# Sliding-window attention into a SwiGLU block: masks by a scan, loads further ahead and tied to the score matmuls, an order of the opening written anew

## The chip, the core and the metric

The kernel runs on one core of a Trainium2 chip. The metric is the time of one execution on the device in microseconds (us), here the median of 16 runs. The core has engines that run side by side, each with its own queue of instructions: TensorE (PE; its weight loads are shown as PEld), VectorE (DVE), ScalarE (ACT), GpSimd (POOL) and SyncE (SP). POOL, SP and ACT also issue DMAs. Engines wait for each other through semaphores, and each works its queue off in order: an instruction that waits holds up all that stand behind it.

## The reference

q, k and v have 8 batches, 8 heads, 576 positions and head size 64. Attention is causal with a window of 64:

```
scores = q @ k^T / 8        kept where 0 <= i - j < 64, else -1e9
attn   = exp(scores - max) / sum;   x = attn @ v     -> as 4608 tokens x 512
out    = (silu(x @ w_gate) * (x @ w_val)) @ w_out    w_gate, w_val: 512 x 1536, w_out: 1536 x 512
```

Inputs and output are float32; the kernel works in bf16 with float32 sums, and may do so.

## The kernel before

The 4608 tokens are cut into 36 attention chunks n of 128 tokens and 9 chunks c of 512 tokens for the SwiGLU block. A chunk n passes through these steps, each a method of the class:

- `load(n)` (line 271): POOL issues three DMAs (six where a chunk crosses a batch) that fetch k, q and v from memory and cast them to bf16: `kn`, `qn` (rings of `NQ` = 6) and `va` (a ring of `NV` = 10). The weights come the same way (`load_w`, `load_wo`).
- the transposes of k and q, which need the head dimension on the partitions. For chunks 0 to 7 PE does them (`first_T`, `Tpe`) and DVE and ACT copy the results out of PSUM; from chunk 8 on `T(n, "k")` and `T(n, "q")` (line 323) are DMA transposes that SP issues. k ends in `kT`, which holds all tokens; q in `qT`, a ring of `NZ` = 8.
- `shift_v(n)`: two DMAs on SP (or DVE copies at the start) that place v shifted by 64 rows, `vb`.
- `S(n)` (line 339): 16 small matmuls for the scores into two PSUM banks, then exp on ACT and, if no bias is used, a multiplication with `mask` on DVE. For chunks 0 to 3 (`bias=True`) two matmuls with `nmask` (0 or -30000) put the mask into PSUM instead.
- `AV(n)`: attention times v, into two banks; DVE divides (`rc`, `xb`).
- `X(n)` (line 402): x is transposed into `xT`, by a DMA transpose on SP, or, with `eng` "act" or "dve", by PE into a bank that this engine copies out.

`F(c, f, lo, hi)` is one of 12 steps of the SwiGLU block: four matmuls of x with a block of w_gate, tanh on ACT, four with a block of w_val, and two DVE operations that write `hT` (silu is made from tanh; the factor is 0.5). At the opening F works on halves of 256 tokens (lo to hi), as soon as two chunks of x are there. `O(c, u)` is 12 matmuls of `hT` with w_out, a copy on ACT and a store. PSUM has eight banks: F rotates over 0 to 3, O uses 4, and all of attention and of PE's transposes ("a") rotates over 5 to 7; `banks()` changes a rotation.

The order of work is written out by hand. `opening()` and `build()` call these methods one after the other; that order is the order on every engine's queue. `_Graph` adds a semaphore wait wherever an operation needs data of, or overwrites data that is still read by, an earlier one. From `for c in range(2, NFC)` on (line 708) the order is a loop of 28 steps u: three F, an AV, a T, an X, an S, an O and a load six chunks ahead. Each group of 12 F closes with four chunks of x, and F(c, 0) needs all four.

The masks are built in `init()` and `init_mask` (line 261): DVE fills `nmask` and `mask` with a constant, and POOL cuts the window with two affine selects and a memset each, in its queue between the DMA issues.

Of the kernel before, what the change touches and what calls it, by code (L numbers as in the profile page):

```python
# [149 lines left out]
class _Kernel:  # L150
    NQ = 6
# [14 lines left out]
    def alloc(self):  # L166
# [21 lines left out]
        self.wz = sb("wz", 512)  # L188
        self.pt = [t[:, :].rearrange("p (h x) -> p h x", h=H) for t in ring("pt", self.NP, H * 192)]
# [47 lines left out]
    def init(self):  # L237
        g = self.g
        self.zero(self.wup[:, :], ["wup"])
        g.op("act", lambda e: e.activation(self.wup[:, :], self.wup[:, :], ACTF.Exp), writes=["wup"])  # L240
        self.zero(self.ident[:, :], ["ident"])
        self.zero(self.wz[:, :], ["wz"])
        self.zero(self.nmask[:, :], ["nmask"])
        self.init_va(0, 4)
        self.zero(self.kT[:, :, 0:64], [("kT", -1, 0), ("kT", -1, 1)])
        self.zero(self.vb[0][0:64, :, 0:66], [("vb", 0, 0)])
        for i in range(self.NP):
            self.zero(self.pt[i][:, :, 64:128], [("pt", i, 0), ("pt", i, 1)])
        self.zero(self.mask[:, :], ["mask"], 1.0)
        self.init_va(4, self.NV)  # L250

# [9 lines left out]
    def init_mask(self, m, key, fill):  # L261
        mm = m[:, :].rearrange("p (a q) -> p a q", a=4)
        self.g.op("pool", lambda e: e.affine_select(
            out=mm, in_=mm, compare_op=ALU.is_gt, fill=fill, base=0,
            pattern=[[0, 4], [-1, 64]], channel_multiplier=1), writes=[key])
        self.g.op("pool", lambda e: e.affine_select(
            out=mm, in_=mm, compare_op=ALU.is_ge, fill=fill, base=64,
            pattern=[[0, 4], [1, 64]], channel_multiplier=-1), writes=[key])
        self.g.op("pool", lambda e: e.memset(m[0:64, 128:192], fill), writes=[key])

    def load(self, n, what="kqv"):
        if n >= NCH:
            return
        parts = list(self.segs(128 * n, 128))
        for x in what:
# [7 lines left out]
            for j, (r, b, s, L) in enumerate(parts):  # L283
                d = dst[r:r + L, :, 0:64]
                a = src[b, :, s:s + L, :].rearrange("h p d -> p h d")
                ks = [(nm, i, j)] if len(parts) > 1 else [(nm, i, 0), (nm, i, 1)]
                self.g.op("pool", lambda e, d=d, a=a: e.dma_start(d, a), writes=ks, dma=True)  # L287
# [51 lines left out]
    def S(self, n, bias=False):  # L339
# [26 lines left out]
        g.op("pe", pe, reads=rd, writes=[b[1] for b in bx])  # L366
# [210 lines left out]
    def opening(self):  # L577
        W = lambda a, b: (self.load_w("g", a, b), self.load_w("v", a, b))
        g = self.g
        self.first_loads()  # L580
        self.init()
        self.init_ident(self.ident, "ident")
# [3 lines left out]
        self.init_mask(self.nmask, "nmask", -30000.0)  # L586
# [4 lines left out]
        W(2, 3)  # L591
        W(3, 4)
        self.init_mask(self.mask, "mask", 0.0)
# [7 lines left out]
        self.load(6)  # L601
        self.load(7)
        self.load_wo(0, 6)
        self.load_wo(6, 12)
        for n in range(4, 8):
            self.shift_v(n)
# [15 lines left out]
        self.AV(1)  # L622
        self.banks("a", [5, 6, 7, 4])
        self.X(0, "act")
        self.S(2, True)
        self.X(1, "dve")
        self.shift_v(2, "dve")
        self.F(0, 0, 0, 256)
        self.AV(2)
        self.Tpe(3, ("dve", "act"))  # L630
        self.F(0, 1, 0, 256)
        self.X(2, "act")
        self.S(3, True)
        self.shift_v(3, "dve")
        self.F(0, 2, 0, 256)
        self.F(0, 3, 0, 256)
        self.AV(3)
        self.F(0, 4, 0, 256)
        self.X(3, "act")
        self.F(0, 5, 0, 256)  # L640
        for f in range(6):
            self.F(0, f, 256, 512)

    def build(self):
        self.opening()
        self.banks("a", [5, 6, 7])
# [16 lines left out]
        for n in (8, 9, 10):  # L663
            self.load(n)
        for n in (8, 9, 10):
            self.T(n, "k")
            self.T(n, "q")
            self.shift_v(n)
        for f in range(0, 8):
            self.F(1, f, 0, 256)  # L670
            if f == 0:
                self.S(6)
            if f == 2:
                self.AV(6)
                self.S(7)
            if f == 4:
                self.X(6, "act")
                self.AV(7)
            if f == 6:
                self.X(7, "act")  # L680
        for f in range(0, 8):
            self.F(1, f, 256, 512)
            if f == 1:
                self.load(11)
            if f == 4:
                self.O(0, 0)
                self.S(8)
            if f == 5:
                self.O(0, 1)
                self.load(12)  # L690
            if f == 6:
                self.AV(8)
                self.X(8)
        self.S(9)
        self.load(13)
        for u in range(4):
            self.F(1, 8 + u)
            self.T(11 + u, "k")
            if u < 2:
                self.O(0, 2 + u)  # L700
            if u < 3:
                self.AV(9 + u)
                self.X(9 + u)
                self.S(10 + u)
            self.T(11 + u, "q")
            self.shift_v(11 + u)
            self.load(14 + u)
        for c in range(2, NFC):
            for u in range(4):
# [7 lines left out]
                self.load(n + 6)  # L717
                self.F(c, 3 * u + 1)
                self.S(n + 1)
                late = c == NFC - 1 and u == 3  # L720
# [52 lines left out]
```

## Time and profile before

| | |
|---|---|
| median of 16 runs | 358.28 us (355.09 to 360.06) |
| profiled execution, its own time | 357.74 us |
| span, from first to last instruction of it | 356.0 us |
| PE busy | 330.4 us, 93% of the span |
| DVE busy | 222.7 us, 63% |
| ACT busy | 136.7 us, 38% |
| POOL busy | 115.0 us, 32% (issuing DMAs of this queue counts as busy) |
| mean granted TensorE clock | 0.981 |

The profile gives for each engine the busy time, and for groups of instructions the mean duration of one, the idle time of the engine before them and what ended it. The timeline lists instructions in order of time, and writes [idle before <-releaser] behind those that the engine stood still for. "Issue to landing" of a DMA is the time from its issue until its data are there. Times inside the profile are counted from the start of the span.

### The profile page before, as it was taken

The numbers are of one execution on the slowest core, as the hardware profiler recorded it, in microseconds if no ns is written. First come the engines' busy times: TensorE is split into PE (matmuls) and PEld (weight loads), VectorE is DVE, ScalarE is ACT, GpSimd is POOL, SyncE is SP. The second block draws the span as 40 slices with busy tenths as digits, with TensorE's granted clock in tenths as the row PEclk, the third lists the DMA queues.
The fourth block names the chain that finished last, engine by engine and source line by source line (L and its number), as shares of the span: only waits on it lengthen the run. The fifth ranks groups of instructions, "written<-read, shape, count | busy, mean of one in ns | idle before, by whom it ended". The sixth has DMA issues, their size and how long they took to land.

```text
span 356.0 us, 6815 instructions
## 1 busy us (share of the span) xinstructions
PE 330.4 (93%) x2648; PEld 174.2 (49%) x2689; DVE 222.7 (63%) x493; ACT 136.7 (38%) x248; POOL 115.0 (32%) x147
## 2 busy tenths in 40 slices
PE   7899879985769999999999999999999999999996
PEld 2677458652334444444444444444444444444443
DVE  8778878463536666666666666666666666555520
ACT  3555445332314444433333333333444334332321
POOL 8999976521453433232323422210000000000000
PEclk9899999998789999999999999999999999999999
DMA  9999999999999999999999999894433321110012
GB/s 175 150 157 181 182 210 157 157 195 167 181 165 168 143 147 138 123 143 135 149 145 139 153 139 154 126 142 99 96 93 92 94 55 44 64 41 29 31 57 92
DMA packets 177600, 45.47 MB, mean 128 GB/s; under 512 B 162144, under 2 KB 173088, under 8 KB 177568
## 3 DMA queue, kind: packets, MB, share of 16 engines
q0 software_dynamic: 119424, 18.36, 77.9%
q1 hardware_dynamic: 51920, 16.84, 28.1%
q10 hardware_dynamic: 6224, 9.83, 8.1%
q8 instruction: 21, 0.34, 0.4%
q14 instruction: 11, 0.09, 0.1%
HBM read 37.75 MB, written 9.44 MB: 133 GB/s over the span
## 4 chain that ended last, share of the span: by engine, by line
PE 83%; DVE 7%; ACT 4%; DMA 3%; issue 3%; ACTq 0%; DVEq 0%
PE ps L496 48%; PE ps L542 26%; PE ps L359 3%; DVE uu L515 2%; DVE xb L399 2%; ACT sig L507 2%; DMA xT<-xb 2%; PE ps L390 2%; PE ps L389 2%; DMA hT<-in_k_dram 1%; DVE hT L518 1%; ACT pt L372 1%; PE ps L564 1%; PE ps L418 1%; PE ps L353 1%
## 5 line engine op out<-in xcount | busy, mean ns | idle before, releaser
L515 DVE SCALAR_TENSOR_TENSOR uu<-sig,ps 128x512 bf16<-128x512 bf16 (+1 forms) x122 | 76.0, 623 | 93.9 <-ACT sig L507 93.5
L496 PE MATMUL ps<-xT,Wg 128*128 128x512 bf16 (+1 forms) x474 | 112.3, 358 | 6.0 <-DMA xT<-xb 3.7
L496 PE MATMUL ps<-xT,Wv 128*128 128x512 bf16 (+1 forms) x476 | 114.8, 359 | 1.4 <-DMA Wv<-in_moe_w_val_dram 0.8
L507 ACT ACTIVATE sig<-ps 128x512 bf16<-128x512 f32 (+1 forms) x122 | 66.9, 549 | 101.2 <-PE ps L496 101.1
L542 PE MATMUL ps<-Wo,hT 128*128 128x512 bf16 x405 | 94.1, 379 | 1.4 <-issue 1.0
L518 DVE SCALAR_TENSOR_TENSOR hT<-uu,ps 128x512 bf16<-128x512 bf16 (+1 forms) x122 | 76.3, 626 | 5.0 <-PE ps L496 0.8
L496 PEld LDWEIGHTS ps<-xT,Wv 128*128 128x128 bf16 x488 | 48.2, 99 | 48.2 <-issue 2.2
L496 PEld LDWEIGHTS ps<-xT,Wg 128*128 128x128 bf16 x488 | 44.8, 99 | 44.4 <-DMA xT<-xb 4.2
L287 POOL DMA_DIRECT2D qn<-in_q_dram x38 | 33.9, 897 | 88.3 <-DMA qT<-qn 88.3
L542 PEld LDWEIGHTS ps<-Wo,hT 128*128 128x128 bf16 x420 | 39.2, 98 | 44.9
L372 ACT ACTIVATE pt<-ps 128x512 bf16<-128x512 f32 x72 | 39.0, 595 | 30.0 <-PE ps L359 29.6
L547 ACT ACTIVATE ost<-ps 128x512 f32<-128x512 f32 x35 | 20.9, 597 | 67.1 <-PE ps L542 67.1
L287 POOL DMA_DIRECT2D kn<-in_k_dram x38 | 34.2, 903 | 27.5 <-DMA kT<-kn 26.1
L287 POOL DMA_DIRECT2D va<-in_v_dram x40 | 35.9, 902 | 3.4 <-DMA Wo<-in_moe_w_out_dram 2.6
L399 DVE TENSOR_TENSOR xb<-ps,rc 128x256 bf16<-128x256 f32 x72 | 30.6, 424 | 2.5
L374 DVE TENSOR_TENSOR pt<-pt,mask 128x512 bf16<-128x512 bf16 x64 | 24.9, 420 | 10.6 <-ACT pt L372 10.1
L390 PE MATMUL ps<-va,pt 128*128 128x65 bf16 x288 | 23.4, 196 | 0.0
L389 PE MATMUL ps<-vb,pt 128*128 128x65 bf16 x288 | 23.3, 196 | 0.0
L389 PEld LDWEIGHTS ps<-vb,pt 128*128 128x128 bf16 x288 | 21.0, 100 | 4.0 <-issue 0.6
L359 PE MATMUL ps<-qT,kT 64*128 64x64 bf16 x576 | 14.9, 192 | 7.6 <-issue 4.0
L390 PEld LDWEIGHTS ps<-va,pt 128*128 128x128 bf16 x288 | 19.7, 100 | 3.7 <-issue 0.5
L359 PEld LDWEIGHTS ps<-qT,kT 64*128 64x128 bf16 x576 | 10.6, 95 | 21.0 <-DVE rc L396 10.4
(51 smaller groups left out, 88.0 us busy)
## 6 DMA issues: line engine op xcount, KB each, us to landing
out_dram<-ost ACTq DMA_DIRECT2D x35, 256.0 KB, 3.1
vb<-va SPq DMA_DIRECT2D x63, 80.0 KB, 4.6
va<-in_v_dram POOLq DMA_DIRECT2D x32, 128.0 KB, 6.2
kn<-in_k_dram POOLq DMA_DIRECT2D x30, 128.0 KB, 6.4
qn<-in_q_dram POOLq DMA_DIRECT2D x30, 128.0 KB, 5.4
Wo<-in_moe_w_out_dram POOLq DMA_DIRECT2D x2, 768.0 KB, 13.9
Wg<-in_moe_w_gate_dram POOLq DMA_DIRECT2D x6, 128.0 KB, 4.6
Wv<-in_moe_w_val_dram POOLq DMA_DIRECT2D x6, 128.0 KB, 4.6
```

The costliest lines, as they stand in the source:

```text
L287: self.g.op("pool", lambda e, d=d, a=a: e.dma_start(d, a), writes=ks, dma=True)
L359: r = e.matmul(sv[p][:, w, c], self.kT[ps, c, k0:k0 + 128], self.qT[ps, c, self.qs(n, 64 * w, 64 * w + 64)], start=not bias, stop=not bias ...
L372: g.op("act", lambda e, po=po, p=p: e.activation(po, sv[p], ACTF.Exp, scale=SCALE), reads=[bx[p][1]], writes=[pk])
L374: g.op("dve", lambda e, po=po: e.tensor_tensor(po, po, m, ALU.mult), reads=[pk, "mask"], writes=[pk])
L389: e.matmul(av[:, j, :], pt[:, h, 0:128], vb[:, h, 0:65], start=True, stop=False)
L390: r = e.matmul(av[:, j, :], pt[:, h, 64:192], va[:, h, 0:65], start=False, stop=True)
L399: g.op("dve", lambda e, xo=xo, av=av, rb=rb: e.tensor_tensor(xo, av[:, :, 0:64], rb, ALU.mult), reads=[bk, ("rc", ir)], writes=[("xb", ix, ...
L496: r = e.matmul(bank[:, lo:hi], W[:, kk, f * 128:f * 128 + 128], xT[:, kk, lo:hi], start=(kk == 0), stop=(kk == NK - 1))
L507: self.g.op("act", lambda e: e.activation(sig[:, lo:hi], G[:, lo:hi], ACTF.Tanh, scale=0.5), reads=[gk], writes=[("sig", i)])
L515: g.op("dve", lambda e: e.scalar_tensor_tensor(uu[:, lo:hi], sig[:, lo:hi], 1.0, G[:, lo:hi], ALU.add, ALU.mult), reads=[("sig", i), gk], ...
L518: g.op("dve", lambda e: e.scalar_tensor_tensor(hT[:, f, lo:hi], uu[:, lo:hi], 0.5, V[:, lo:hi], ALU.mult, ALU.mult), reads=[("uu", i), vk] ...
L542: r = e.matmul(OB[:, :], hT[:, f, 128 * u:128 * u + 128], self.Wo[:, f, :], start=(f == 0), stop=(f == NF - 1))
```

## The change

- **Masks.** `nmask` and `mask` are no longer made on POOL. DVE makes a running sum along each row of the identity (a scan), takes the difference of two halves of it, clears one corner, and makes `nmask` from `mask` by one more operation. Two memsets on DVE go.
- **Weights.** Blocks 2 and 3 of each gate matrix come with one DMA instead of two.
- **Opening.** The order of X, F, S and Tpe in the first 512 tokens is another; X(0), X(1) and F(0,0) come ahead of S(2), X(3) stands behind F(0,5). The loads 6 and 7, w_out and the shifts of v 4 to 7 stand later in the text, but in the same order on POOL and SP.
- **Banks.** The attention rotation keeps four banks (5, 6, 7, 4) until X(7), after which O takes bank 4.
- **Chunks 8 to 14.** `load(11)` follows 8, 9 and 10 at once; the transposes of k and q and the shifts of 8 to 11 follow each other on SP with no X between them. X(8) to X(11) are done by PE and ACT instead of DMA transposes. The second half of c = 1 is written out by hand.
- **Loads 12 and later.** `load(n, after=m)` makes the DMAs wait until PE has done S(m); a new key ("S", n) that S writes carries it. In the loop load(n + 6) stands behind S(n + 1) and waits for it.
- **Rings.** `NQ` goes from 6 to 4.

```diff
@@ -148,7 +148,7 @@
 
 
 class _Kernel:
-    NQ = 6
+    NQ = 4
     NV = 10
     NZ = 8
     NP = 4
@@ -186,6 +186,7 @@
         self.kT = sb("kT", 4 * (T + 64))[:, :].rearrange("p (c t) -> p c t", c=4)
         self.qT = sb("qT", 4 * self.NZ * 128)[:, :].rearrange("p (c t) -> p c t", c=4)
         self.wz = sb("wz", 512)
+        self.cum = sb("cum", 128)
         self.pt = [t[:, :].rearrange("p (h x) -> p h x", h=H) for t in ring("pt", self.NP, H * 192)]
         self.rc = ring("rc", 4, 4, F32)
         self.xb = ring("xb", 4, DM)
@@ -239,15 +240,28 @@
         self.zero(self.wup[:, :], ["wup"])
         g.op("act", lambda e: e.activation(self.wup[:, :], self.wup[:, :], ACTF.Exp), writes=["wup"])
         self.zero(self.ident[:, :], ["ident"])
+        self.init_ident(self.ident, "ident")
         self.zero(self.wz[:, :], ["wz"])
-        self.zero(self.nmask[:, :], ["nmask"])
         self.init_va(0, 4)
         self.zero(self.kT[:, :, 0:64], [("kT", -1, 0), ("kT", -1, 1)])
         self.zero(self.vb[0][0:64, :, 0:66], [("vb", 0, 0)])
+        self.init_mask()
         for i in range(self.NP):
             self.zero(self.pt[i][:, :, 64:128], [("pt", i, 0), ("pt", i, 1)])
-        self.zero(self.mask[:, :], ["mask"], 1.0)
         self.init_va(4, self.NV)
+
+    def init_mask(self):
+        g = self.g
+        cum = self.cum
+        g.op("dve", lambda e: e.tensor_tensor_scan(cum[:, :], self.wz[:, 0:128], self.ident[:, :], 0.0, ALU.add, ALU.add),
+             reads=["wz", "ident"], writes=["cum"])
+        mm = self.mask[:, :].rearrange("p (a q) -> p a q", a=4)
+        hi = cum[:, 64:128].unsqueeze(1).to_broadcast([128, 4, 64])
+        lo = cum[:, 0:64].unsqueeze(1).to_broadcast([128, 4, 64])
+        g.op("dve", lambda e: e.tensor_tensor(mm, hi, lo, ALU.subtract), reads=["cum"], writes=["mask"])
+        g.op("dve", lambda e: e.memset(self.mask[0:64, 128:192], 0.0), reads=["mask"], writes=["mask"])
+        g.op("dve", lambda e: e.tensor_scalar(self.nmask[:, :], self.mask[:, :], -1.0, 30000.0, ALU.add, ALU.mult),
+             reads=["mask"], writes=["nmask"])
 
     def init_va(self, a, b):
         for i in range(a, b):
@@ -258,19 +272,10 @@
             out=m[:, :], in_=m[:, :], compare_op=ALU.not_equal, fill=1.0, base=0,
             pattern=[[-1, 128]], channel_multiplier=1), writes=[key])
 
-    def init_mask(self, m, key, fill):
-        mm = m[:, :].rearrange("p (a q) -> p a q", a=4)
-        self.g.op("pool", lambda e: e.affine_select(
-            out=mm, in_=mm, compare_op=ALU.is_gt, fill=fill, base=0,
-            pattern=[[0, 4], [-1, 64]], channel_multiplier=1), writes=[key])
-        self.g.op("pool", lambda e: e.affine_select(
-            out=mm, in_=mm, compare_op=ALU.is_ge, fill=fill, base=64,
-            pattern=[[0, 4], [1, 64]], channel_multiplier=-1), writes=[key])
-        self.g.op("pool", lambda e: e.memset(m[0:64, 128:192], fill), writes=[key])
-
-    def load(self, n, what="kqv"):
+    def load(self, n, what="kqv", after=None):
         if n >= NCH:
             return
+        gate = [] if after is None else [("S", after)]
         parts = list(self.segs(128 * n, 128))
         for x in what:
             src = {"k": self.k, "q": self.q, "v": self.v}[x]
@@ -284,7 +289,7 @@
                 d = dst[r:r + L, :, 0:64]
                 a = src[b, :, s:s + L, :].rearrange("h p d -> p h d")
                 ks = [(nm, i, j)] if len(parts) > 1 else [(nm, i, 0), (nm, i, 1)]
-                self.g.op("pool", lambda e, d=d, a=a: e.dma_start(d, a), writes=ks, dma=True)
+                self.g.op("pool", lambda e, d=d, a=a: e.dma_start(d, a), reads=gate, writes=ks, dma=True)
 
     def shift_v(self, n, eng="sp"):
         if n >= NCH:
@@ -363,7 +368,7 @@
 
         rd = [("kT", m, b) for m in (n - 1, n) for b in range(2)] + [("qT", iz, b) for b in range(2)]
         rd += ["nmask", "ident"] if bias else []
-        g.op("pe", pe, reads=rd, writes=[b[1] for b in bx])
+        g.op("pe", pe, reads=rd, writes=[b[1] for b in bx] + [("S", n)])
         m = self.mask[:, :].rearrange("p (a q) -> p a q", a=4)[:, self.var(n)]
         m = m.unsqueeze(2).to_broadcast([128, 2, 4, 64])
         for p in range(2):
@@ -576,21 +581,16 @@
 
     def opening(self):
         W = lambda a, b: (self.load_w("g", a, b), self.load_w("v", a, b))
-        g = self.g
         self.first_loads()
         self.init()
-        self.init_ident(self.ident, "ident")
         self.load(0, "v")
         self.load(1, "v")
         self.load(2, "kq")
-        self.init_mask(self.nmask, "nmask", -30000.0)
         W(0, 1)
         self.load(2, "v")
         self.load(3, "kqv")
         W(1, 2)
-        W(2, 3)
-        W(3, 4)
-        self.init_mask(self.mask, "mask", 0.0)
+        W(2, 4)
         W(4, 6)
         self.load(4)
         W(6, 8)
@@ -598,12 +598,6 @@
         W(8, 9)
         W(9, 10)
         W(10, 12)
-        self.load(6)
-        self.load(7)
-        self.load_wo(0, 6)
-        self.load_wo(6, 12)
-        for n in range(4, 8):
-            self.shift_v(n)
 
         self.banks("a", [0, 1, 2, 3, 5, 6, 7])
         self.warm(11)
@@ -620,30 +614,40 @@
         self.AV(0)
         self.Tpe(2, ("dve", "act"))
         self.AV(1)
+        self.X(0, "act")
+        self.X(1, "dve")
+        self.F(0, 0, 0, 256)
         self.banks("a", [5, 6, 7, 4])
-        self.X(0, "act")
         self.S(2, True)
-        self.X(1, "dve")
         self.shift_v(2, "dve")
-        self.F(0, 0, 0, 256)
+        self.Tpe(3, ("dve", "act"))
+        self.load(6)
+        self.load(7)
+        self.load_wo(0, 6)
+        self.load_wo(6, 12)
+        for n in range(4, 8):
+            self.shift_v(n)
+        self.F(0, 1, 0, 256)
         self.AV(2)
-        self.Tpe(3, ("dve", "act"))
-        self.F(0, 1, 0, 256)
-        self.X(2, "act")
         self.S(3, True)
         self.shift_v(3, "dve")
         self.F(0, 2, 0, 256)
+        self.X(2, "act")
         self.F(0, 3, 0, 256)
         self.AV(3)
         self.F(0, 4, 0, 256)
+        self.F(0, 5, 0, 256)
         self.X(3, "act")
-        self.F(0, 5, 0, 256)
         for f in range(6):
             self.F(0, f, 256, 512)
 
+    def T8(self, n):
+        self.T(n, "k")
+        self.T(n, "q")
+        self.shift_v(n)
+
     def build(self):
         self.opening()
-        self.banks("a", [5, 6, 7])
         self.Tpe(4, ("dve", "act"))
         self.F(0, 6)
         self.S(4)
@@ -660,51 +664,61 @@
         self.F(0, 11)
         self.Tpe(6, ("dve", "act"))
         self.Tpe(7, ("dve", "act"))
-        for n in (8, 9, 10):
+        for n in (8, 9, 10, 11):
             self.load(n)
-        for n in (8, 9, 10):
-            self.T(n, "k")
-            self.T(n, "q")
-            self.shift_v(n)
-        for f in range(0, 8):
-            self.F(1, f, 0, 256)
-            if f == 0:
-                self.S(6)
-            if f == 2:
-                self.AV(6)
-                self.S(7)
-            if f == 4:
-                self.X(6, "act")
-                self.AV(7)
-            if f == 6:
-                self.X(7, "act")
-        for f in range(0, 8):
-            self.F(1, f, 256, 512)
-            if f == 1:
-                self.load(11)
-            if f == 4:
-                self.O(0, 0)
-                self.S(8)
-            if f == 5:
-                self.O(0, 1)
-                self.load(12)
-            if f == 6:
-                self.AV(8)
-                self.X(8)
+        for n in (8, 9, 10, 11):
+            self.T8(n)
+        F1 = lambda *fs: [self.F(1, f, 0, 256) for f in fs]
+        F1(0)
+        self.S(6)
+        F1(1, 2)
+        self.AV(6)
+        F1(3)
+        self.S(7)
+        F1(4)
+        self.X(6, "act")
+        F1(5)
+        self.AV(7)
+        F1(6, 7)
+        self.X(7, "act")
+        self.banks("a", [5, 6, 7])
+        self.banks("o", [4])
+        F1 = lambda *fs: [self.F(1, f, 256, 512) for f in fs]
+        F1(0, 1)
+        self.O(0, 0)
+        self.S(8)
+        self.load(12, after=8)
+        F1(2, 3)
+        self.AV(8)
+        F1(4)
+        self.O(0, 1)
+        self.X(8, "act")
         self.S(9)
-        self.load(13)
-        for u in range(4):
-            self.F(1, 8 + u)
-            self.T(11 + u, "k")
-            if u < 2:
-                self.O(0, 2 + u)
-            if u < 3:
-                self.AV(9 + u)
-                self.X(9 + u)
-                self.S(10 + u)
-            self.T(11 + u, "q")
-            self.shift_v(11 + u)
-            self.load(14 + u)
+        self.load(13, after=9)
+        self.T8(12)
+        F1(5, 6)
+        self.AV(9)
+        F1(7)
+        self.X(9, "act")
+        self.S(10)
+        self.load(14, after=10)
+        self.T8(13)
+        self.O(0, 2)
+        self.AV(10)
+        self.F(1, 8)
+        self.X(10, "act")
+        self.S(11)
+        self.load(15, after=11)
+        self.F(1, 9)
+        self.AV(11)
+        self.T8(14)
+        self.F(1, 10)
+        self.X(11, "act")
+        self.S(12)
+        self.load(16, after=11)
+        self.load(17, after=12)
+        self.O(0, 3)
+        self.F(1, 11)
         for c in range(2, NFC):
             for u in range(4):
                 n = 4 * c + u + 4
@@ -714,9 +728,9 @@
                 self.X(n)
                 self.T(n + 3, "q")
                 self.shift_v(n + 3)
-                self.load(n + 6)
                 self.F(c, 3 * u + 1)
                 self.S(n + 1)
+                self.load(n + 6, after=n + 1)
                 late = c == NFC - 1 and u == 3
                 if not late:
                     self.O(c - 1, u)
```

## The prediction

> **What bounds the kernel now.** I read the page's slices first, then who waited for whom, then the timelines of PE and SP between 30 and 105 us, last the busy time by stage. The slices:
>
> ```profile
> PE   7899879985769999999999999999999999999996
> PEclk9899999998789999999999999999999999999999
> DMA  9999999999999999999999999894433321110012
> ```
>
> A slice is 8.9 us. From the thirteenth on PE is full: the loop is bound by PE. The dip in the tenth to twelfth (80 to 107 us) is idle PE, and its clock falls there too. The DMA engines are busy until about 220 us, but in the loop nobody on PE waits for them. The waits (who <- whom: us, times, longest):
>
> ```profile
> PE ps L359 <- issue: 4.0, 1, 4.0
> PE ps L496 <- DMA xT<-xb: 3.7, 1, 3.7
> PE ps L359 <- DVE xb L399: 2.6, 3, 1.4
> PE ps L472 <- DVE xb L399: 1.1, 1, 1.1
> PE ps L472 <- DVE kT L232: 0.9, 1, 0.9
> PE ps L496 <- DMA Wv<-in_moe_w_val_dram: 0.8, 1, 0.8
> POOL qn L287 <- DMA qT<-qn: 88.3, 20, 7.8
> ```
>
> The first is named "issue", so its cause is to be looked for in time: PE, then SP's queue.
>
> ```profile
> 88.64 0.61 PE L359 MATMUL ps<-qT,kT 64*128 64x64 bf16 x16 [4.02 <-issue]
> 100.60 1.03 PE L496 MATMUL ps<-xT,Wg 128*128 128x512 bf16 x2 [3.75 <-DMA xT<-xb]
> ...
> 75.25 1.27 SPq L331 DMA_TRANSPOSE kT<-kn  x1
> 79.82 1.43 SPq L411 DMA_TRANSPOSE xT<-xb  x1
> 81.30 1.28 SPq L331 DMA_TRANSPOSE qT<-qn  x1
> ```
>
> S(11) starts at 88.64. SP issued its q transpose at 81.30, which took 7.25 us to land: 88.55. The raw q of chunk 11 had landed at 67.2; its transpose stood behind X(9), which SP could not issue before 79.82, when DVE had x. So the 4.02 us are a place in SP's queue. The 3.75 are X(11): issued at 94.70, landed 5.85 later, and F(2,0) needs it. The stages:
>
> ```profile
> 59.52:102.17 42.65, 31.81 (x289) 18.99 (x293) 21.46 (x53) 12.97 (x27) 14.01 (x16) 0.90 1.95 170
> 110.87:145.67 34.80, 34.43 (x268) 16.84 (x272) 22.92 (x48) 13.87 (x25) 11.99 (x15) 1.00 1.41 147
> ```
>
> The columns are length, busy PE, PEld, DVE, ACT, POOL, clock, DMA share, GB/s. The second row is the loop's first group: PE 34.43 of 34.80. A step is 8.70 us (F(2,3) starts at 110.87, F(2,6) at 119.57), and from F(2,3) to the end are 356.0 - 110.87 = 245.13 us, which the change doesn't shorten. Run back at full pace, F(2,0) would begin at 110.87 - 8.70 = 102.17. The whole question is where this mark comes to stand.
>
> **The change part by part.**
>
> *Masks on DVE.* DVE's last memset ends at 4.65 and it waits 0.80 us for k's first load. Added: a scan of 128x128 (no row shows one; between 0.15, a memset of this size, and 0.84, twice the 0.42 of a 128x256 read of PSUM; I take 0.35, since a scan depends on itself along the row), a difference of 128x256 (0.2 to 0.42, the mask product of 128x512; 0.3), a corner (0.1), a tensor_scalar of 128x256 (0.15 to 0.42; 0.3): 1.05. Removed: memsets of 0.17 and 0.27. Net +0.6, under the 0.80: nothing. At the upper ends (1.8) it is +1.35, and S(0), at 8.34, starts 0.55 late. POOL's identity is ready at 1.56, before the scan could start.
>
> *POOL's queue.* It loses two mask groups (5.40 to 6.84 and 16.35 to 17.64: 2.7 us) and two weight issues (0.73 each): 4.2 us at most for all loads behind. Here a rule speaks against the change: the Trainium skill, "DMA: Bandwidth & Descriptors", section "Issuing engines are not separate DMA queues", says that all issuers share the same 16 DMA engines, and that starting elsewhere saves only sequencer time, small beside the transfer. With full engines the 4.2 us would move no landing. The row: the landings behind POOL are spaced 0.73 to 0.85 us for 128 KB, 1.37 for 256 KB, but around the pauses there are gaps of 1.03 (9.49 to 10.52), 1.94 (11.24 to 13.18) and 2.29 (20.23 to 22.52): 0.3 + 1.1 + 0.9 = 2.3 us in which nothing came. So I move every landing behind by 2.1, between 0 by the rule and 4.2. By the rule the sum below loses 1.2 us (S(8)).
>
> *Opening, 8.34 to 31.08.* Wv of f = 4 lands at 23.89 now; 2 us earlier it is there, and F(0,4) takes 0.87 as its neighbours do instead of 2.07 (22.66 to 24.73): -1.2. Moving F(0,0) ahead of S(2) swaps equal work. X(3) now stands directly ahead of the F that needs it, and ACT's copy (0.60 and its latency) is uncovered: +0.75. Sum -0.45.
>
> *Four banks, 31.08 to 59.52.* With three, Tpe(5) waits 1.12 for a bank that DVE frees, Tpe(7) 0.93, S(7) 1.42. With (5, 6, 7, 4) the bank they take was left one use earlier; following the rotation from S(2) on I find none taken too early. Worth -2.05 up to F(1,0). Of the 1.42 little is left, since in this stretch DVE sets the pace (0.8 us per half F, 0.83 per chunk for the masks, 1.1 for xb), and X(7), moved ahead of F(1,0)'s second half, again uncovers a copy: -0.2. So F(1,0)'s second half starts at 59.52 - 0.45 - 2.05 - 0.2 = 56.8.
>
> *From there to F(2,0).* PE's list: 8 half F at 0.87 = 7.0; 4 F at 1.73 = 6.9; 4 O at 2.59 = 10.4; 5 S at 0.35 = 1.75; 4 AV at 0.55 = 2.2; the four new PE transposes at 0.24 = 1.0. Together 29.2. Waits that remain: X(9), because DVE must do the mask of S(9) (1.5 after it), F5, F6 (0.8 each) and xb (1.1) in 4.2 us where PE has 3.2: 1.1; and about 0.1 to 0.3 for each mask that comes just behind its AV: 0.6. Sum 30.9, against 42.65. F(2,0) starts at 56.8 + 30.9 = 87.7. The 5.85 us of X(11) and the wait on T(11) are gone, and with no idle stretch of 4 us the slow matmuls at 88 and 100 us too (two F at 3.3 instead of 1.73: some 3 us of the 11.7).
>
> *Are the transposes there?* SP issues a set T, T, shift, shift in 4.2 us (54.36 to 58.33 for chunk 8), latency 6.7 for q of chunk 8, 8.2 to 8.3 for 9 and 10. Set 8 starts when k of chunk 8 lands: 54.34 - 2.1 = 52.2. q lands at 60.4, 65.9, 70.2, 74.4 for chunks 8 to 11. PE reaches S(8) at 56.8 + 1.75 + 2.59 = 61.2, S(9) at 67.5, S(10) 72.4, S(11) 77.9. Met, with 0.8 us at the first. `NQ` = 4 makes load 10 wait for Tpe(6) at about 44; its landing was 59.19 with a backlog of 15.5, so this is covered.
>
> *The gate.* Load 12 is issued after S(8) at 61.6, three issues and some 6 us to land: 68; transposes of 1.3 and 4.8: 74; S(12) comes at 82. Behind a gated load on POOL only later loads wait; who waits for those is T on SP, and behind T(n+3) stands X(n). In the loop load(n+6) has three steps, 26 us, until SP's T. Covered. POOL's 88.3 us of waiting for qT becomes waiting for S and costs nothing.
>
> *Sum.* 87.7 - 102.17 = -14.5: span 341.5. The profiled execution's own time (357.74) is 1.74 above its span and the median of the runs 0.54 above it: 341.5 + 2.3 = 343.8 us.
>
> **The rivals.**
>
> *The transposes come late.* For: the DMA slices are full until 220 us, and T took up to 8.8 us. If nothing lands earlier, q of chunk 8 lands at 62.45 and S(8) waits 1.2: 345. If the sets follow each other in 6.2 instead of 4.2 us, q of chunk 11 lands at 80.4 and S(11) waits 2.5: 346.3; with both, 82.5 against 77.9: 348.4. Against: four X leave SP, and loads 12 and later are held back just then.
>
> *PE is fuller than I sum.* The mask chain stays covered, the clock doesn't fall at 13 to 18 us, X(9)'s wait is taken by slack: -2.5, 341.
>
> *The gate puts its loads onto X (slower).* In the loop X(4c+3) is issued at 132.51, landed after 4.3 us, and F(3,0) starts 0.2 us later. S(16) ends at the same moment, so the gated k, q and v start together beside X. Four group ends (into c = 3 to 6) have loads. Each us that X lands later costs four; the gain of 14.5 is used up at 3.6 us each, that is a latency of 7.9. For: under load one X took 7.65. Against: the others took 4.1 to 6.4 and loads ran beside X before as well. At 8.3 us: 360.
>
> *It doesn't do what it says.* S and X might be held by something else that ended just behind the transposes. In the trace S(12) waits until 94.61 on its own q (94.52), also in the queue; I see no second wait.
>
> **How the numbers follow.** Forecast 0.6; late transposes 0.22; fuller 0.1; the gate on X 0.06, of which 0.05 end slower and 0.01 within; no effect 0.02. No difference of less than 0.3% can be told. Faster 0.93, same 0.02, slower 0.05. The likeliest gives 343.8; the range from 340 (fuller, and an end of the loop's waits) to 349.5 (late transposes at their upper end) leaves out the gate and the no-effect case.
>
> **What would show it.** F(2,0) at 88 us and F(2,3) at 96; no wait over 2 us of PE behind 20 us; clock 1.00 from there; S(8) with the smallest margin over its q transpose; POOL waiting for the score matmuls instead of qT; a step of 8.70 still. Wrong if S(8) to S(11) wait for DMA, if group ends show waits for xT, or if DVE's first cast starts behind 5.6.

## The result: 343.4 us, 4.05% faster

| | before | after |
|---|---|---|
| median of the runs compared | 358.19 us | 343.40 us (343.36 to 344.05, 9 runs) |
| ratio after / before | | 0.9595, 95% interval 0.9572 to 0.9618 |
| profiled execution, its own time | 357.74 us | 344.03 us |
| span | 356.0 us | 342.2 us |
| tanh of F(2,0), from the span's start | 102.52 | 90.33 |
| F(2,0) to F(3,0), F(3,0) to F(4,0) | 35.53, 35.35 | 34.82, 34.82 |
| F(8,0) to the end | 43.78 | 43.41 |

The three stretches add up to the span's 13.8 us: 12.2 until F(2,0), 1.2 in the first two groups of the loop (0.7 of it is F(2,0) itself, which ran at the lower clock before: 2.92 us from its tanh to the next, 2.21 now; 0.5 is a wait of F(4,0)), 0.4 behind the last F(c, 0). The slices after:

```profile
PE   7889998979999999999999999999999999999996
DMA  9999999999999999999999999999963311100012
```

The dip of PE in the tenth to twelfth slice is gone. The page of this run has no row for the clock; its mean granted clock is given as 1.000 (0.981 before). The DMA engines are as full as before until about 250 us. The waits (who <- whom: us, times, longest):

```profile
POOL kn L292 <- PE ps L364: 126.2, 22, 11.1
PE ps L423 <- DVE xb L404: 3.7, 6, 1.3
```

No wait of PE for a transpose is left (before: 4.0 of S(11), 3.7 of F(2,0)). POOL's 88.3 us of waiting for `qT` is now waiting for the score matmuls (L364), which is the gate, and nobody pays for it. PE's timeline around the places of the prediction:

```profile
73.70 0.40 PE L423 MATMUL ps<-ident,xb 128*128 128x128 bf16 x4 [1.27 <-DVE xb L404]
79.51 0.41 PE L364 MATMUL ps<-qT,kT 64*128 64x64 bf16 x16
89.27 1.03 PE L501 MATMUL ps<-xT,Wg 128*128 128x512 bf16 x4
```

X(9) has the longest wait of PE behind 20 us, 1.27. S(11) and F(2,0) wait for nothing. Stages (length, busy PE, PEld, DVE, ACT, POOL, clock, DMA share, GB/s): from F(1,0)'s second half to F(2,0), and four steps of the loop from F(2,3) on:

```profile
56.74:89.27 32.53, 29.99 (x299) 18.04 (x305) 19.09 (x49) 14.61 (x30) 17.26 (x21) 1.00 1.84 186
97.97:132.79 34.82, 34.45 (x268) 16.87 (x272) 22.93 (x48) 13.89 (x25) 11.85 (x15) 1.00 1.32 141
```

The first stretch was 42.65 long at a clock of 0.90 and is 32.53 at 1.00. The loop's row is as it was.

### The profile page after: what moved, and what is told of

Read it like the earlier page. It is cut to its first block, busy times and chain, and to the rows that moved or that the text cites. A ratio compares the mean times of both kernels' runs of the same rounds, so it can differ in the third digit from the quotient of the medians.

```text
span 342.2 us, 6800 instructions
## 1 busy us (share of the span) xinstructions
PE 327.6 (96%) x2664; PEld 172.3 (50%) x2705; DVE 222.6 (65%) x495; ACT 138.1 (40%) x252; POOL 111.6 (33%) x139
## 4 chain that ended last, share of the span: by engine, by line
PE 83%; DVE 8%; ACT 4%; issue 2%; DMA 1%; ACTq 0%
PE ps L501 48%; PE ps L547 27%; DVE uu L520 3%; PE ps L364 3%; DVE xb L404 2%; PE ps L394 2%; PE ps L395 2%; ACT pt L377 1%; DMA hT<-in_k_dram 1%; ACT sig L512 1%; DVE hT L523 1%; PE ps L569 1%; PE ps L423 1%; ACT xT L231 1%; DVE rc L401 1%
## 5 line engine op out<-in xcount | busy, mean ns | idle before, releaser
L501 PE MATMUL ps<-xT,Wg 128*128 128x512 bf16 (+1 forms) x477 | 111.0, 354 | 2.9 <-DVE uu L520 1.7
L501 PE MATMUL ps<-xT,Wv 128*128 128x512 bf16 (+1 forms) x475 | 112.7, 354 | 0.9 <-DMA Wv<-in_moe_w_val_dram 0.2
L292 POOL DMA_DIRECT2D kn<-in_k_dram x38 | 33.3, 880 | 132.0 <-PE ps L364 126.2
L501 PEld LDWEIGHTS ps<-xT,Wv 128*128 128x128 bf16 x488 | 47.2, 98 | 46.7 <-DMA Wv<-in_moe_w_val_dram 0.5
L394 PEld LDWEIGHTS ps<-vb,pt 128*128 128x128 bf16 x288 | 20.2, 98 | 4.6 <-DVE pt L379 1.2
L395 PEld LDWEIGHTS ps<-va,pt 128*128 128x128 bf16 x288 | 19.0, 97 | 3.3
L364 PEld LDWEIGHTS ps<-qT,kT 64*128 64x128 bf16 x576 | 10.4, 95 | 13.2 <-DVE rc L401 9.7
L364 PE MATMUL ps<-qT,kT 64*128 64x64 bf16 x576 | 14.7, 191 | 0.0
```

The source lines that it names most:

```text
L292: self.g.op("pool", lambda e, d=d, a=a: e.dma_start(d, a), reads=gate, writes=ks, dma=True)
L364: r = e.matmul(sv[p][:, w, c], self.kT[ps, c, k0:k0 + 128], self.qT[ps, c, self.qs(n, 64 * w, 64 * w + 64)], start=not bias, stop=not bias ...
L394: e.matmul(av[:, j, :], pt[:, h, 0:128], vb[:, h, 0:65], start=True, stop=False)
L395: r = e.matmul(av[:, j, :], pt[:, h, 64:192], va[:, h, 0:65], start=False, stop=True)
L501: r = e.matmul(bank[:, lo:hi], W[:, kk, f * 128:f * 128 + 128], xT[:, kk, lo:hi], start=(kk == 0), stop=(kk == NK - 1))
```

## The experiments

My theory after the result: PE stood behind a series of waits, for banks, for S(11) and for X(11), and the change takes all of them away; the gate is free. Rivals: one part does it all and the others are decoration; the clock does part of it by itself; the gate harms or helps. Eight runs take one thing out of the changed kernel or move it, four add one thing to the kernel before. The new order of the opening, `NQ` and the early load(11) were not taken back alone, so what each of them is worth is not shown. Landings and issue times below are those of the DMA records; "the mark" is the tanh of F(2,0), at 102.52 before and 90.33 after.

### X(8) to X(11) as DMA transposes

X(8) to X(11) go back to SP as DMA transposes; the cut shows X(8), the other three change alike:

```diff
-        self.X(8, "act")
+        self.X(8)
```

> The changed kernel with X(8) to X(11) as DMA transposes on SP again, behind the same T sets. My theory (S(11)'s wait of 4.0 us was the place in the queue; X on PE is worth only what X(11) still costs): PE loses four transposes (1.0 us) and the wait of X(9) (1.3), and F(2,0) waits for X(11), issued at about 82 and landed 6 us later: F(2,0) at 88 to 91, 342.5 to 345. Rival (X on PE is worth the whole 3.75 us of F(2,0)'s wait and more, as X also delays T(12) to T(14)): 347 or more.

Measured: 353.84 us, ratio to before 0.9848 (0.9808 to 0.9888), the mark at 98.46. PE, then SP's queue:

```profile
96.53 1.89 PE L501 MATMUL ps<-xT,Wg 128*128 128x512 bf16 x4 [9.38 <-DMA xT<-xb]
```

```profile
85.79 1.27 SPq L336 DMA_TRANSPOSE qT<-qn  x1
87.69 1.13 SPq L309 DMA_DIRECT2D vb<-va  x2
88.91 1.44 SPq L416 DMA_TRANSPOSE xT<-xb  x1
```

I expected next to nothing, and that fell; the rival's "347 or more" came true. x of chunk 11 was there at about 83, but X(11) stands behind the set T of chunk 14, whose loads wait for the gate and land at 83.03, 85.73 and 87.67. X was issued at 88.91 and took 7.6 us. The next run keeps the DMA and puts T(13) behind X(10), and in the same way T(14) behind X(11):

```diff
         self.load(14, after=10)
-        self.T8(13)
         self.O(0, 2)
         self.AV(10)
         self.F(1, 8)
-        self.X(10, "act")
+        self.X(10)
+        self.T8(13)
```

> The changed kernel with X(8) to X(11) as DMA transposes, as in the run before at 353.8, but T(13) placed behind X(10) and T(14) behind X(11) on SP. My theory for the 353.8 (X(11) was ready at 83 and issued at 88.9, since T(13) and T(14) ahead of it waited for gated loads): X(11) is issued at 83 and lands 7.6 later, F(2,0) at 90.5 to 92 instead of 97.6, 345 to 347. Rival (the place on SP is innocent, the DMA engines are full there and X lands late wherever it stands): F(2,0) behind 95, 351 or more.

Measured: 348.36 us, ratio 0.9722 (0.9673 to 0.977), the mark at 93.81. X(11) is issued at 83.76 and lands at 91.84:

```profile
91.89 1.46 PE L501 MATMUL ps<-xT,Wg 128*128 128x512 bf16 x3 [4.73 <-DMA xT<-xb]
```

So of the 10.4 us that the DMA transposes cost, 5.5 are the place in SP's queue, and 5.0 are left with the place mended, where F(2,0) waits 4.73 us for a transfer of 8.1.

### The same X on PE, close behind AV

Here X(8) to X(11) stay on PE, but each directly behind its AV, with the F and O that lay between now behind it (for X(8); 9 to 11 likewise).

```diff
         self.AV(8)
+        self.X(8, "act")
         F1(4)
         self.O(0, 1)
-        self.X(8, "act")
```

> The changed kernel with X(8) to X(11) on PE directly behind their AV, no F or O between. My theory for the small gain of X on PE alone in the kernel before (its four X stood directly behind AV and PE waited 2.14, 1.04, 1.04 and 2.04 us for DVE's xb): the waits come here too, 4 to 6 us in place of 1.6: F(2,0) 2.5 to 4.5 us later than 89.3, 346 to 348. Rival (that part gained little because its loads had no gate, not because of the place of X): within 0.7 us of the changed kernel, 343 to 344.2.

Measured: 352.99 us, ratio 0.9854 (0.9792 to 0.9917): nearly as bad as by DMA, and much worse than I expected. The waits for x, and a stage:

```profile
PE ps L423 <- DVE xb L404: 9.6, 8, 2.3
```

```profile
56.70:70.00 13.30, 10.91 (x92) 7.16 (x93) 6.37 (x18) 3.99 (x10) 2.63 (x3) 0.87 1.75 176
```

The waits went from 3.7 to 9.6 us (X(8) to X(11): 2.26, 2.25, 1.04, 1.90), which is 5.9 of the 8.95 us by which the mark is late. The rest is the clock: 0.87 here and 0.83 from 90 to 100 us, 1.00 in both stretches after. O(0,1) takes 3.2 instead of 2.6 us, the half F(1,4) 1.7 instead of 0.9, and 10 us at 0.83 do 1.7 us less of work: together about 3. I had counted the waits and not the clock behind them. What makes a PE transpose cheap is the work between AV and X: it covers DVE's 1.2 us of divisions and what DVE still has ahead of them (behind AV(8) it first works off two half F, until 65.45, and divides from 65.37 to 66.55).

### The gate off

```diff
-        gate = [] if after is None else [("S", after)]
+        gate = []
```

> The changed kernel without the gate: loads 12 and later wait only for their buffers. My theory (the gain lies before F(2,0): place in SP's queue, X on PE, banks; the gate only keeps loads off X): load 12 is issued when T(8) has landed (58.7 instead of 62.0), nothing before F(2,0) moves; in the loop X lands later than 2.5 us, between 4 and 5.5 as before the change, which is just met at the group ends: 343.4 to 345, F(2,0) within 0.3 us of 89.3. Rival (the gate makes room on the DMA engines and T(8) to T(11) land in time only because of it): S(9) to S(11) wait 2 us or more, 346 or more.

Measured: 345.07 us (344.43 to 346.56), ratio 0.9622 (0.9587 to 0.9657), the mark at 90.37, unmoved. The loss is in the loop: groups of 35.21, 35.92, 34.82 and 35.84. F(4,0), and the transposes of x in the first six steps of the loop (shortest, median, longest from issue to landing), without the gate and then with it:

```profile
160.44 1.02 PE L501 MATMUL ps<-xT,Wg 128*128 128x512 bf16 x4 [0.94 <-DVE uu L520]
```

```profile
DMA to landing us min/median/max: 4.8/5.8/6.7
```

```profile
DMA to landing us min/median/max: 2.5/2.5/3.6
```

The wait is put down to DVE, but the X that F(4,0) needs lands at 160.34, 0.1 ahead of its start. Over all steps that have loads, to about 240 us, X takes 2.9 us in the median with the gate (2.4 to 4.4) and 4.9 without (2.9 to 6.7). The gate does not hold the loads until X has landed; it changes which is issued first. Without the gate, then with it:

```profile
101.84 0.87 POOL L292 DMA_DIRECT2D qn<-in_q_dram  x1 [4.20 <-DMA qT<-qn]
102.24 1.20 SPq L416 DMA_TRANSPOSE xT<-xb  x1
```

```profile
102.20 1.19 SPq L416 DMA_TRANSPOSE xT<-xb  x1
102.88 0.89 POOL L292 DMA_DIRECT2D kn<-in_k_dram  x1 [6.05 <-PE ps L364]
```

Without it a load is issued 0.4 us ahead of X, with it the first one 0.7 us behind. X then lands at 104.77 instead of 108.89, with the loads still running beside it. Why so small a lead is enough stays open. In the kernel before the same six steps gave 4.3/5.4/7.6; F(4,0) paid 0.5 us for it, and F(3,0), which began 0.17 behind the landing of its X, nothing. The medians of the runs differ by 1.7 us; all four runs without the gate lie above all nine with it, while the intervals of the two ratios to before overlap.

### The gate alone, in the kernel before

```diff
                 self.shift_v(n + 3)
-                self.load(n + 6)
                 self.F(c, 3 * u + 1)
                 self.S(n + 1)
+                self.load(n + 6, after=n + 1)
```

> The kernel before with the gate alone, in the loop from load 18 on (placed behind S(n + 1) and waiting for it). My theory after the run without a gate: X lands in about 2.5 instead of 4.3 to 7.6 us, the two long groups of the loop (35.53 and 35.35 instead of 34.82) become 34.82, nothing else moves: 1 to 1.5 us less, 356.8 to 358 against 358.2 to 359. Rival (the gate helps only where X is already off SP before the loop): no difference within 0.3 us, group lengths as before.

Measured: 355.3 us (353.02 to 356.71) against 358.92, ratio 0.9903 (0.9873 to 0.9933). In the profile the first two groups are 34.82, X takes 2.4 us in the median of the first six steps, and the mark is at 102.14. The groups make 1.2 of the 1.6 us by which this span is shorter. Only 0.5 of that is the wait for X that I expected (F(4,0)); 0.7 is F(2,0) at full clock.

"Nothing else moves" did not hold. The opening of this profile ran 2.8 us late, at weights that the gate does not touch (waits of 1.98 and 0.74 us around 24 us), and still the mark was not late: S(11) waits 1.15 instead of 4.02 us for a q that lands at the same time as before (88.45, before 88.55), and X(11) takes 3.7 instead of 5.85 us. Load 18, which was issued at 92.76 before, just ahead of X(11), now comes at 106.00. The medians differ by 3.6 us. The 2.1 us of X(11) would explain most of the 2 us that the span does not show, but there is no profile with the gate and an undisturbed opening, so this stays an estimate.

### Three banks

```diff
     def build(self):
         self.opening()
+        self.banks("a", [5, 6, 7])
         self.Tpe(4, ("dve", "act"))
```

> The changed kernel with the attention rotation on banks 5, 6, 7 from Tpe(4) on, as before the change. My theory: the waits of 1.12 (Tpe(5)), 0.93 (Tpe(7)) and part of 1.42 us (S(7)) come back: F(1,0) at 47.9 instead of 45.84, time 345.4 to 346.2. Rival (DVE sets the pace there anyway and the banks cost nothing): 343.4 to 344.

Measured: 346.53 us (346.51 to 346.57), ratio 0.9657 (0.9626 to 0.9687), the mark at 92.80, 2.5 late. The waits of Tpe(5), Tpe(7) and S(7) are back:

```profile
PE ps L477 <- DVE xb L404: 1.1, 1, 1.1
PE ps L477 <- DVE kT L233: 0.9, 1, 0.9
PE ps L364 <- DVE xb L404: 0.6, 1, 0.6
```

The first two are the sizes of before (1.1, 0.9); S(7) waits 0.6 instead of 1.4, because the new order puts F(1,3) between.

### Masks and weight blocks 2 and 3 on POOL as before

The scan's `init_mask` gives way to the old one:

```diff
-        self.init_mask()
...
+        self.init_mask(self.nmask, "nmask", -30000.0)
...
-        W(2, 4)
+        W(2, 3)
+        W(3, 4)
+        self.init_mask(self.mask, "mask", 0.0)
```

> The changed kernel with both masks made by POOL again and the weight blocks 2 and 3 in two DMAs each. My theory (the queue behind POOL has idle landings of 2.3 us at these pauses): all landings behind come 2 to 2.5 us later, F(0,4) waits about 1 us for its weights again, q of chunk 8 lands at 62 instead of 59.9, and S(8) waits: together 1 to 1.5 us, 344.4 to 345. Rival (the 16 DMA engines are full, so POOL's time moves no landing): landings within 0.7 us, 343.4 to 343.9.

Measured: 345.4 us (345.07 to 347.01), ratio 0.9634 (0.96 to 0.9668), the mark at 91.62, 1.3 late. k of chunk 8 lands at 54.74 instead of 51.32 and q's transpose at 62.85 instead of 59.93:

```profile
62.90 0.41 PE L362 MATMUL ps<-qT,kT 64*128 64x64 bf16 x16 [1.14 <-DMA qT<-qn]
```

S(8) waits 1.14 here. This is the 1.2 us that the prediction gave to the case in which no landing moves. The opening is slower as well: F(1,0)'s tanh comes 0.5 us later than in the changed kernel. The span is 1.3 us longer, the median 2.0. The masks and the two weight issues were put back together, so their shares are not told apart.

### Single parts in the kernel before

The transposes T of chunks 8 to 11 on SP in one row, load 11 early (both loops over n, of loads and of T; 12 to 14 then follow in the steps):

```diff
-        for n in (8, 9, 10):
+        for n in (8, 9, 10, 11):
```

> The kernel before with one part of the change: load 11 follows 8 to 10, and the T sets of 8 to 11 stand together on SP; X(8) to X(11) stay DMA transposes. My theory (S(11)'s wait of 4.0 us is its place behind X(9)): the wait goes and the slow clock behind it (1.5), X(11) is still waited for: F(2,0) 4 to 5.5 us earlier, 353 to 354.5. Rival (SP and the DMA engines are full, so the time only moves into F(2,0)'s wait for X(11)): 356.5 to 358.5.

Measured: 357.33 against 358.92 us, ratio 0.9967 (0.9932 to 1.0001). S(11)'s wait is gone (0.49, for DVE), but X(11) is issued at 90.87 and takes 8.5 us:

```profile
99.45 1.89 PE L496 MATMUL ps<-xT,Wg 128*128 128x512 bf16 x4 [8.36 <-DMA xT<-xb]
```

The 4.0 us moved into F(2,0)'s wait, which went from 3.75 to 8.36. The mark is 1.1 earlier.

X(8) to X(11) on PE, directly behind AV, which is where they stand in that kernel (X(8) as well):

```diff
-                self.X(9 + u)
+                self.X(9 + u, "act")
```

> The kernel before with another part: X(8) to X(11) on PE and ACT; T, loads and rings as before. My theory: taking X out of SP's queue ends both waits, since nothing stands ahead of T(11, q) any more and F(2,0) needs no DMA: 4.0 and 3.75 us and about 3 of slow clock go, 1.0 of PE work and 1.3 of waits for xb come: 348.5 to 350.5, nearly what the four parts together give there. Rival (both parts are needed, each ends only its own wait): 353 to 355.

Measured: 356.14 against 358.92 us, ratio 0.9903 (0.987 to 0.9936). The row of waits for x:

```profile
PE ps L418 <- DVE xb L399: 6.6, 5, 2.1
```

Both waits for DMA are gone and the mark is 4.4 earlier, at 98.08; I had expected 8 to 10 in all. 6.3 us come back as waits of X(8) to X(11) for DVE (2.14, 1.04, 1.04, 2.04), much as in the close variant above. In the loop F(3,0) waits 2.01, by the profile for DVE, but its last X lands at 133.92 and it starts at 134.01: beside ungated loads X took 6.6 us, and that group is 37.83 long.

The clock: dummy matmuls on zeros, extra work whose result nobody reads, fill the two long waits, 16 ahead of S(11) and 14 ahead of F(2,0):

```diff
+                if u == 1:
+                    self.warm(16)
                 self.S(10 + u)
...
+                if c == 2 and u == 0:
+                    self.warm(14)
```

> The kernel before with matmuls on zeros ahead of S(11) (16 of 128x512, 3.5 us) and of F(2,0) (14, 3.0 us): extra work in the two long waits, nothing else. If the slow matmuls behind the waits come from PE's idle time: F(1,10) takes 1.73 instead of 3.2 us and F(2,0) too, clock 1.00 there; X(11) is issued 1.5 earlier, so F(2,0) starts 1.5 and ends 3 us earlier: 355 to 356.5. Rival (the clock falls for another reason, or the wait for X only grows by what is saved): no difference, 358 to 359.5.

Measured: 357.48 against 357.98 us, ratio 1.0007 (0.9973 to 1.004), mean clock 1.000 instead of 0.981.

```profile
84.34 3.63 PE L486 MATMUL ps<-wz 128*128 128x512 bf16 x16 [0.20 <-ACT ost L547]
94.34 0.41 PE L359 MATMUL ps<-qT,kT 64*128 64x64 bf16 x16 [3.46 <-DMA qT<-qn]
101.00 1.04 PE L496 MATMUL ps<-xT,Wg 128*128 128x512 bf16 x4 [1.39 <-DMA xT<-xb]
```

F(1,9) and what follows run at full pace, but S(12) then stands 3.46 us for its own q, which lands at 94.25, and F(2,0) begins at 101.00 instead of 100.60: X(11) was issued 2.0 us earlier (92.74) and landed 0.4 us later (100.95). The slow clock of before was worth nothing by itself there: DMA landings set the end of that stretch.

### Two tries to get below 343.4

Another order of the second half of c = 1 (one more half F ahead of AV(8) and AV(9), F(1,8) in halves, O(0,2) and O(0,3) moved):

```diff
+        self.F(1, 8, 0, 256)
...
-        F1(2, 3)
+        F1(2, 3, 4)
...
-        F1(5, 6)
+        F1(5, 6, 7)
...
-        F1(7)
+        self.O(0, 2)
```

> The changed kernel with another order of the second half of c = 1: half of F(1, 8) behind X(7), which covers its copy; F(1, 4) ahead of AV(8); F(1, 7) ahead of AV(9) and O(0, 2) between AV(9) and X(9); S(11) ahead of AV(10), so that F or O stands between each S and AV, AV and X. If the rest of the waits there is order alone: 0.69 at X(7), 0.9 at AV(8), 1.27 at X(9), 0.31 at X(11) go, 0.4 of DVE work for the halves comes: 1.5 to 2.5 us less than the changed kernel, 341 to 342. If DVE sets the pace there, the waits move and it is within 0.5 us of it.

Measured: 343.89 us (343.22 to 343.91), ratio 0.9611 (0.9572 to 0.9649); the mark at 89.97. The waits of PE in the stretch are 0.80, 1.07, 0.65 and 0.38 at other places, for DVE and ACT. No gain: the second case, in which DVE sets the pace and the waits move.

In the last run only ACT's order is touched. With `hold` O issues its matmuls alone, and `out()` its copy and store; O(0,0) is held behind S(8) in the same way:

```diff
-        self.O(0, 1)
+        out = self.O(0, 1, hold=True)
         self.X(8, "act")
         self.S(9)
+        out()
```

> The changed kernel with one thing moved on ACT alone: the copies of the first two output tiles, O(0,0) and O(0,1), are issued behind the exponentials of S(8) and S(9) instead of ahead of them (PE, DVE, SP and POOL keep their order). Theory (what my sum under-sized was ACT's order: the exponentials stand behind a copy of 0.60 us and its DMA issue, so the masks come late and AV(8) takes 0.96 and AV(9) 1.21 us instead of 0.49): AV(8) and AV(9) take 0.5 to 0.65, X(9) doesn't wait longer than its 1.27, F(2,0)'s tanh comes 0.7 to 1.2 us earlier than at 90.33, median 342.2 to 342.8. Rival (DVE sets the pace there: from 70.06 to 74.4 it is never idle, and what the AVs gain comes back as wait of X(9)): X(9) waits 1.8 to 2.4, F(2,0) within 0.3 us of 90.33, median 343.1 to 343.8.

Measured: 344.19 us (343.72 to 346.15), ratio 0.9617 (0.957 to 0.9663). The masks of S(8) and S(9) are done 0.7 and 0.8 us sooner after the start of their S, but the copy now stands ahead of the tanh of the next F:

```profile
63.83 0.61 PE L501 MATMUL ps<-xT,Wg 128*128 128x256 bf16 x4 [0.63 <-DVE uu L520]
71.12 0.61 PE L501 MATMUL ps<-xT,Wg 128*128 128x256 bf16 x4 [0.73 <-DVE uu L520]
```

F(1,4) and F(1,7) wait 0.63 and 0.73 for a bank, X(9) its 1.28 as before. From F(1,0)'s second half to the mark it takes 33.4 us instead of 32.9. This is neither what I expected nor the rival's waits; the mark, at 90.10, is near the rival's number only because the opening of this profile was 0.7 us faster. What the masks gained came back at another place.

## Why the prediction was right, point by point

**The sum.** Predicted span 341.5, measured 342.2. Two terms missed and cancelled in part: F(2,0) came at 89.27 instead of 87.7 (+1.6), and from F(2,3) (97.97) to the end it took 244.2 instead of 245.1 us (-0.9). The median lies 1.2 above the span instead of 2.3, and so ended at 343.4 against 343.8. That the two are so close is luck; the errors of +1.6, -0.9 and -1.1 us happen to cancel.

**Opening, banks.** F(1,0)'s first half at 45.84 (45.93 predicted), its second at 56.74 (56.8). Here too errors cancel: S(0) began 0.27 late, from there to Tpe(4) the 0.45 of the sum came in full (22.29 us instead of 22.74), and from Tpe(4) to F(1,0) it was 2.4 us less instead of 2.05 (14.94 instead of 17.35). The run with three banks gives this stretch back: 2.4 at F(1,0), 2.5 at the mark, 3.1 in the median.

**Masks on DVE.** The rows of DVE after:

```profile
2.14 0.35 DVE L256 TENSOR_TENSOR_SCAN cum<-wz,ident 128x128 bf16<-128x128 bf16 x1
2.53 0.29 DVE L261 TENSOR_TENSOR mask<-cum 128x256 bf16<-128x256 bf16 x1
3.00 0.66 DVE L263 TENSOR_SCALAR nmask<-mask 128x256 bf16<-128x256 bf16 x1
5.69 1.47 DVE L233 CAST ost<-hT 128x1024 bf16<-128x1024 f32 x2 [0.52 <-DMA hT<-in_k_dram]
```

The scan took the 0.35 assumed, the difference 0.29 (0.3). The tensor_scalar lasted 0.66, twice my value, but the next memset starts 0.39 behind it. The first cast starts at 5.69, behind the 5.6 that I named as a sign against me; the sign was badly chosen. DVE still stood idle for 0.52, so k's load was late (it landed at 5.67, before at 5.43), not DVE.

**POOL's queue.** I moved landings by 2.1 us; those of chunks 6 and 8 moved by 3.3 and 3.0. By the Trainium skill ("DMA: Bandwidth & Descriptors", "Issuing engines are not separate DMA queues") only sequencer time is saved, which is usually small beside the transfer. Here it was not small: with the work back on POOL k of chunk 8 is issued 4.1 us later (38.49 instead of 34.39) and lands 3.4 us later, which costs 1.3 us of the span and 2.0 of the median.

**Transposes in time.** q landed at 59.93, 65.40, 68.06 and 72.53, against 60.4, 65.9, 70.2 and 74.4. S(8) at 61.18 (61.2 predicted) had the smallest margin, 1.25, as named. The rival of late transposes did not come true, but only this margin kept it away: in the run with the masks on POOL S(8) waits.

**The PE list, 30.9 predicted, 32.53 measured.** This is the term that was too small. AV(8) and AV(9) take 0.96 and 1.21 us from the end of the F ahead to the start of the F behind, where an AV with its mask ready takes 0.49: 1.2 us of waiting for masks against 0.6 in the sum. The PE transposes take 0.32 each instead of 0.24 (+0.3), X(9) waits 1.27 instead of 1.1, X(11) 0.31 instead of nothing, and three gaps of 0.16 in issue were left out; against that, an AV that is ready takes 0.49 and not 0.55 (-0.2). Together 1.6. I blamed ACT's order for the masks; the run that changes this order did not bear it out. That the chain of ACT and DVE is full between 60 and 75 us is argued from the two last runs, not shown for each part.

**The gate, "costs nothing".** The step failed in the good direction. I had it as a rival that would push loads onto X and be slower; the runs show the opposite: X in 2.5 us instead of 5.4 to 5.8 in the first six steps, and 1.7 us lost with the gate off. The prediction read the loop before as free of waits for DMA. F(4,0) did wait, 0.5 us until its X landed at 172.25; the profile calls most of it "issue". That is 0.5 of the 0.9 us by which my "unchanged" loop became shorter. The other 0.4 lies behind F(8,0), where the kernel without the gate is as short (43.42), so it is not the gate's; its cause stays open.

**X on PE, "two waits gone".** Right in its result, but the prediction did not say how much hangs on the place. The same PE transposes directly behind AV lose 9.6 us.

**The clock.** I put 3 of the 11.7 us down to slow matmuls. The run with dummy matmuls shows that in the kernel before this time is not added to the waits: at full clock the waits for landings grow by it. In the close variant, where PE waits for DVE and no landing, the lower clock did cost about 3 us.

## What to carry to other kernels

Waits in series hide each other: three parts were worth 0.3% to 1.0% each alone, all together 4.05%, so follow the chain past the wait that you remove, to what lands or comes free next. A transpose moved from DMA to PE needs cover between its input and itself as much as the DMA needed lead; count the cover in microseconds of PE work. In a queue worked off in order look at what is ahead of a late item, and have bulk loads issued behind, not ahead of, a transfer that the next step waits for.

## What was not expected of the hardware

- The transpose of x (one DMA from SP) takes 2.9 us in the median of the gated loop while it has loads (2.4 to 4.4), 4.9 without the gate, and up to 8.5 in the kernel before with T of chunks 8 to 11 in one row. What the gate changes is a lead of 0.7 us at the issue.
- PE's granted clock can fall after waits of only 1.9 to 2.3 us. In the close variant it fell at X(8)'s 2.26 and X(11)'s 1.90, but not at X(9)'s 2.25. By the Trainium skill ("TensorE: Matmul & The Clock Gate", "HAM oscillation — how this bites in real kernels") gaps over about 3.4 us are the rule for a fall; the section behind it, "A second HAM failure mode: psum-queue depth-cycling", tells of a kernel that fell by frequent small idles. The clock records of these profiles tell the cases apart. All 13 that have such records change the clock only at multiples of 3.41 us, on a grid of their own. Counted on that grid, from 20 us on, full clock was followed by half clock wherever PE was idle for 1.90 us or more within one stretch, and never where it was 1.78 or less. X(8)'s wait lies in one stretch, X(9)'s is split over two (length, busy PE, ..., clock):

```profile
63.02:66.43 3.41, 1.27 (x21) 0.75 (x18) 3.21 (x10) 0.95 (x3) 1.64 (x2) 1.00 1.41 183
66.43:69.84 3.41, 3.23 (x15) 2.07 (x16) 0.97 (x3) 0.98 (x2) 0.00 (x0) 0.50 1.86 222
73.26:76.67 3.41, 1.77 (x25) 1.21 (x23) 2.79 (x9) 1.46 (x4) 3.41 (x6) 1.00 1.15 186
76.67:80.08 3.41, 2.73 (x34) 1.81 (x35) 1.85 (x6) 1.95 (x4) 0.75 (x2) 1.00 1.45 119
```

- POOL's own work in the first 18 us (two mask groups and two issues, 4.2 us) still moved an issue at 34 us by 4.1 us, and its landing at 51 us by 3.4: POOL had no pause in between that could have taken it up.
